# Sigmoid attention with its keys in chunks of 128 and the last 64 of two pairs taken together

## The chip, the cores and the metric

The kernel runs on one core of a Trainium2 chip. The metric is device time in microseconds (us) of one execution; 1193.59 us is the median of three runs of the kernel before. Engines are named as the profile names them: PE (matmul), PEld (its weight loads), DVE, ACT, POOL, and SP, which here only issues DMAs. SPq and ACTq are the DMA issues of SP and ACT.

## What is computed

```python
# q, k, v: (4, 12, 448, 64) fp32
scores = (q @ k.transpose(0, 1, 3, 2)) / sqrt(64) - log(448)
attn   = 1 / (1 + exp(-scores))
x      = (attn @ v), heads side by side         # (4, 448, 768)
# first block, weights float64
u  = x + (x.T @ U @ V).T                         # rank 32 over the 448 positions
x  = u + relu(u @ w_ch1) @ w_ch2                 # 768 -> 3072 -> 768
# second block
t  = x @ w_theta
u  = x + w_tok_r @ (x * cos(t)) + w_tok_i @ (x * sin(t))
out = u + relu(u @ w_ch)
```

## The kernel before

The result stays in SBUF as `X`, transposed (feature on the partition). Nearly every product is made of three matmuls of two-part fp32r numbers (high by high, high by low, low by high); the attention's weights times values, the U product and the transposes are plain fp32.

**Attention.** The 48 heads are taken as 24 pairs, p = 0 to 23, six to a batch. The loop over p is written out by hand, and every engine gets its instructions in that order. For pair p it does: scores `QK(p, 0)` and `QK(p, 1)`, two chunks of 112 keys each; for each chunk six matmuls, two heads on the two halves of PE's rows, and one sigmoid on ACT (tile `A`). Between them stand `AV(p-1, c)`, weights times values of the pair before (fp32, two heads on the two halves of PE's columns, four chunks, one PSUM accumulator `av`), the transposes `TK`, `TQ` of the next pair's k and q on DVE with their splits (`kh`, `kl`, `qh`, `ql`), `XN(p-2)`, which turns a finished pair of `X` for the rank-32 product, and after each sixth pair `U1` (that product) and then `U2` (its second half, two matmuls for a PSUM tile `h` and one addition into `X`, in three of the next six iterations).

**Loads.** At the end of iteration p SP gets the loads of pair p+4's k and q (four DMAs each, because each is loaded as four sets of 32 x 32 squares, `load_squares`) and of pair p+3's v (two DMAs). Only the very first q and the first two v go by ACT's queue. Each DMA waits for the landing of the DMA that stands eight places before it in the program (eight completion counters are dealt in turn, over both queues), and its buffer must be free.

**Weights.** They come as float64, are loaded as 32-bit words by SP (tile `ws`), and `Conv` makes two fp32r parts of them in steps: `size` on ACT, `shift`, `sign`, `low` on DVE, then `fin` (a copy on ACT, `ca_w` and `w` on POOL). Nine conversions are dealt into the attention loop (`early_step`), the rest into the mixer (`place`, `tick`).

**The rest** is the channel mixer `ch1`/`ch2` over 12 blocks of 256 hidden features and four batches, then the second block: 5,000 matmuls of 384 or 448 columns in a row.

Of the kernel before, what the change touches and what calls it, by code (L numbers as in the profile page):

```python
# [24 lines left out]
def tile_kernel(  # L25
# [88 lines left out]
    def add_pool(o, a, b):  # L114
        nc.gpsimd.tensor_add(o, a, b)

# [10 lines left out]
    class Conv:  # L127
        def __init__(self, key, pp, n, dma, fin, turns=False, more=()):
            self.key, self.pp, self.n, self.dma = key, pp, n, dma
            self.turns = turns  # L130
# [6 lines left out]
        def load(self):  # L137
            self.S = cv.tile([P, DM, 2], U32, tag="ws", name=f"ws_{self.key}", bufs=3)[:self.pp, :self.n]
            self.hw = self.S[:, :, 1]
            self.dma(self.S)  # L140

        def size(self):
# [3 lines left out]
            nc.scalar.activation(f(self.A), f(self.hw), AF.Abs, scale=65536.0)  # L146

        def shift(self):
            A = self.A
            nc.vector.tensor_scalar(  # L150
                out=f(A), in0=f(A), scalar1=2.0, scalar2=1.875 * 2.0 ** 32, op0=ALU.max, op1=ALU.min
            )
            nc.vector.tensor_scalar(
                out=A, in0=A, scalar1=4, scalar2=1, op0=ALU.logical_shift_left, op1=ALU.logical_shift_right
            )

        def sign(self):
            A, hw = self.A, self.hw
            nc.vector.scalar_tensor_tensor(
                out=A, in0=hw, scalar=0x80000000, in1=A, op0=ALU.bitwise_and, op1=ALU.bitwise_or  # L160
            )
            nc.vector.tensor_scalar(out=hw, in0=A, scalar1=0xFF800000, scalar2=None, op0=ALU.bitwise_and)

        def low(self):
            A, e = f(self.A), f(self.hw)
            c = 2.0 ** -52 * (INV_HI if self.turns else 1.0)
            nc.vector.scalar_tensor_tensor(
                out=e, in0=self.S[:, :, 0], scalar=c, in1=e, op0=ALU.mult, op1=ALU.mult
            )
            if self.turns:  # L170
                nc.vector.scalar_tensor_tensor(
                    out=e, in0=A, scalar=INV_LO, in1=e, op0=ALU.mult, op1=ALU.add
                )
                nc.scalar.activation(A, A, AF.Copy, scale=INV_HI)
# [6 lines left out]
    def split(o, a, e, eng=nc.gpsimd):  # L181
        hi_act(o[:, 0], a)
        eng.tensor_sub(a, a, f(o[:, 0]))  # L183
        eng.tensor_add(o[:, 1], a, e)  # L184

    def fin_split(dest, key, name, tag):
        def fin(a, e):
            dest[key] = ring(tag, name)
            split(dest[key], a, e)
# [28 lines left out]
    def conv_kept(name, src, kk, turns):  # L218
        st = {}

        def fin(a, e):
            st["o"] = spill_tile(name).rearrange("p (a n) -> p a n", a=2)
            split(st["o"].bitcast(F32R), a, e, nc.vector if turns else nc.gpsimd)
# [11 lines left out]
    def conv_tok(i):  # L235
# [17 lines left out]
        def fin(a, e):  # L253
            st["t"] = spill_tile(f"tok{i}")
            st["n"] = st["t"][:CP, 2 * S:2 * S + NC * P]
            add_pool(st["n"], a, e)
# [12 lines left out]
        return Conv(f"tok{i}", CP, NC * P, dma, fin, False, [turn, spill])  # L269

    def conv_U():
        def dma(s):
            sv = s.rearrange("p (a c r) t -> p a c (r t)", a=2, c=NC)
            for par in range(2):
                for c in range(NC):
                    for n, t, m in runs(par, c * CP, (c + 1) * CP):
                        o = n - c * CP
                        nc.sync.dma_start(out=sv[o:o + m, par, c], in_=U_w[t:t + m, :])

        def fin(a, e):  # L280
            add_pool(u_in.rearrange("p a c r -> p (a c r)"), a, e)
        return Conv("U", CP, 2 * NC * R, dma, fin)

    def conv_V(par):
# [8 lines left out]
        def fin(a, e):  # L293
            o = vcat[:, par]
            hi_act(o, a)
            for g in (1, 3):
                sl = slice(g * R, (g + 1) * R)
                lo_pool(a[sl], a[sl], o[sl])
                add_pool(o[sl], a[sl], e[sl])
# [12 lines left out]
    u_in = ap.tile([CP, 2, NC, R], F32, name="u_in")  # L312
    vcat = ap.tile([P, 2, S], F32R, name="vcat")

    q_t, k_t, v_t, qq_t, kk_t, A_t, av_t, xn_t = {}, {}, {}, {}, {}, {}, {}, {}
# [22 lines left out]

    def load_v(p, eng=nc.sync):
        b, hp = divmod(p, NH)  # L340
        vt = ap1.tile([CP, 2, NC, D], F32, tag="v", name=f"v_{p}", bufs=4)
        for h in range(2):
            eng.dma_start(out=vt[:, h], in_=v[b, 2 * hp + h].rearrange("(c p) d -> p c d", p=CP))
        v_t[p] = vt

    def TQ(p):
# [8 lines left out]
        else:  # L355
            hi_act(h_, x)
        qq_t[p] = (h_, l_)
        return lambda: lo_dve(l_, x, h_)

    kT_t = {}  # L360
# [12 lines left out]
    def K_lo(p):  # L373
        h_, l_ = kk_t[p]
        lo_dve(l_, kT_t.pop(p), h_)

    def QK(p, half):


        (kh, kl), (qh, ql) = kk_t[p], qq_t[p]  # L380
        for c in (2 * half, 2 * half + 1):
            ps = ps_b.tile([P, 2, 512], F32, tag="sc", name=f"sc_{p}_{c}", bufs=2)
            for n, (a, b) in enumerate(((kh, qh), (kh, ql), (kl, qh))):
                for h in range(2):
                    sl = slice(h * D, (h + 1) * D)
                    nc.tensor.matmul(  # L386
                        ps[:CP, h, :S], a[sl, c * CP:(c + 1) * CP], b[sl], start=n == 0, stop=n == 2
                    )
            a = ap1.tile([CP, 2, S], F32, tag="A", name=f"A_{p}_{c}", bufs=6)
# [565 lines left out]
```

## Time and profile before

| | |
|---|---|
| timed runs | 1192.83, 1193.59, 1193.81 us |
| the profiled execution | 1195.51 us, of which its span in the trace is 1193.6 us |
| granted clock of PE, mean | 0.998 |
| PE busy | 1177.1 us, 99% of the span |
| DVE, ACT, POOL busy | 783.5, 377.4, 298.1 us |
| DMA, attention stage | 0.73 of the 16 engines' time from 20 to 160 us |

The attention stage ends at about 192 us. A busy PE in the profile is not PE at its peak, since matmuls overlap; how far apart they start tells more than how long one takes.

### The profile page before, as it was taken

The page shows a single profiled execution, that of the slowest core. Times are in us where ns is not written, and L with a number is a line of the kernel's source. Part 1 is how long each engine was busy: PE and PEld are TensorE (multiplying, and loading weights), DVE is VectorE, ACT ScalarE, POOL GpSimd, SP SyncE. Part 2 cuts the span into 40 slices and gives each one's busy share as a digit, 9 for nine tenths or more (in the row PEclk, how much of TensorE's full clock was granted, in tenths as well). Part 3 has the DMA queues.
Part 4 walks back from the last instruction along what each step waited for, and adds up shares of the span by engine and source line. Part 5 has one row for each costly group of instructions (what it writes and reads, how often), then busy time and mean ns, then how long its engine had stood idle before and what let it go on. Part 6 is the DMA issues. An engine that isn't in the chain of part 4 may idle for free.

```text
span 1193.6 us, 15586 instructions
## 1 busy us (share of the span) xinstructions
PE 1177.1 (99%) x6220; PEld 1016.0 (85%) x6220; DVE 783.5 (66%) x955; ACT 377.4 (32%) x498; POOL 298.1 (25%) x170
## 2 busy tenths in 40 slices
PE   8989999999999999999999999999999999999998
PEld 4444446999999999999999999999989999999997
DVE  5578874557786778677867796878574642833443
ACT  6767774212221222221222121212124431631110
POOL 0131212422232233222322242525102421320000
PEclk9999999999999999999999999999999999999999
DMA  8687740011232123212321232324442000030344
GB/s 139 118 164 148 154 87 27 1 40 67 95 99 80 53 95 111 69 53 95 110 69 54 95 115 86 118 99 127 188 160 80 1 1 1 2 158 1 51 65 70
DMA packets 190808, 99.88 MB, mean 84 GB/s; under 512 B 158736, under 2 KB 182672, under 8 KB 190608
## 3 DMA queue, kind: packets, MB, share of 16 engines
q1 hardware_dynamic: 164752, 95.45, 28.7%
q10 hardware_dynamic: 25984, 3.44, 2.1%
q8 instruction: 49, 0.80, 0.3%
q14 instruction: 23, 0.19, 0.1%
HBM read 80.71 MB, written 18.15 MB: 83 GB/s over the span
## 4 chain that ended last, share of the span: by engine, by line
PE 90%; DVE 3%; SPq 3%; DMA 2%; ACT 1%; issue 1%; ACTq 0%; DVEq 0%
PE g L626 10%; PE g L627 10%; PE g L628 10%; PE y L648 10%; PE y L650 10%; PE y L649 10%; PE av L399 3%; PE y L837 3%; PE y L838 3%; PE y L836 3%; PE sc L386 3%; PE th L759 2%; PE th L763 2%; PE th L760 2%; PE wc L919 2%; PE wc L917 2%
## 5 line engine op out<-in xcount | busy, mean ns | idle before, releaser
L648 PE MATMUL y<-gh,w 128*128 128x448 f32 x576 | 211.3, 367 | 0.7 <-DVE X L652 0.7
L626 PE MATMUL g<-uh,w 128*128 128x448 f32 x576 | 210.7, 366 | 0.0
L627 PE MATMUL g<-ul,w 128*128 128x448 f32 x576 | 210.5, 365 | 0.0
L650 PE MATMUL y<-gh,w 128*128 128x448 f32 x576 | 210.5, 365 | 0.0
L628 PE MATMUL g<-uh,w 128*128 128x448 f32 x576 | 210.5, 365 | 0.0
L649 PE MATMUL y<-gl,w 128*128 128x448 f32 x576 | 210.4, 365 | 0.0
L652 DVE TENSOR_TENSOR X<-y,X 128x896 f32<-128x896 f32 x144 | 156.4, 1088 | 78.8 <-PE y L650 77.3
L183 POOL TENSOR_TENSOR ca_w<-ca_w,w 128x768 f32<-128x768 f32 x48 | 90.6, 1888 | 456.7 <-ACT w L109 444.2
L633 ACT ACTIVATE gh<-g 128x896 fp32r<-128x896 f32 x48 | 44.2, 920 | 330.7 <-PE g L628 330.7
L634 DVE SCALAR_TENSOR_TENSOR gl<-g,gh 128x896 fp32r<-128x896 f32 x48 | 52.4, 1091 | 100.9 <-ACT gh L633 100.9
L648 PEld LDWEIGHTS y<-gh,w 128*128 128x128 f32 x576 | 108.2, 188 | 9.9 <-issue 1.1
L626 PEld LDWEIGHTS g<-uh,w 128*128 128x128 f32 x576 | 108.2, 188 | 9.1 <-issue 0.4
L650 PEld LDWEIGHTS y<-gh,w 128*128 128x128 f32 x576 | 108.2, 188 | 8.8
L628 PEld LDWEIGHTS g<-uh,w 128*128 128x128 f32 x576 | 108.2, 188 | 8.7
L627 PEld LDWEIGHTS g<-ul,w 128*128 128x128 f32 x576 | 108.2, 188 | 8.7
L649 PEld LDWEIGHTS y<-gl,w 128*128 128x128 f32 x576 | 108.2, 188 | 8.5
L390 ACT ACTIVATE A<-sc,bias_s 112x896 f32<-112x896 f32 x96 | 91.5, 1005 | 22.9 <-PE sc L386 22.7
L184 POOL TENSOR_TENSOR w<-ca_w,ws_w 128x768 fp32r<-128x768 f32 x48 | 96.2, 2004 | 3.8
L399 PE MATMUL av<-A,v 112*64 112x448 f32 x384 | 83.5, 557 | 1.1 <-ACT X L109 1.1
L112 POOL TENSOR_TENSOR zl<-t,zh 128x768 fp32r<-128x768 f32 x23 | 42.7, 1883 | 114.1 <-ACT zh L109 114.1
L146 ACT ACTIVATE ca_w<-ws_w 128x768 f32<-128x768 f32 x48 | 43.5, 906 | 62.3 <-POOL w L184 55.9
L836 PE MATMUL y<-tok,zh 128*128 128x448 f32 x168 | 61.7, 367 | 0.0
(145 smaller groups left out, 1861.6 us busy)
## 6 DMA issues: line engine op xcount, KB each, us to landing
ws_w<-in_moe_w_ch_dram SPq DMA_DIRECT2D x48, 768.0 KB, 4.5
k<-in_k_dram SPq DMA_DIRECT2D x96, 56.0 KB, 2.7
q<-in_q_dram SPq DMA_DIRECT2D x92, 56.0 KB, 2.4
v<-in_v_dram SPq DMA_DIRECT2D x44, 112.0 KB, 2.8
ws_th<-in_moe_w_theta_dram SPq DMA_DIRECT2D x6, 768.0 KB, 4.4
th_d<-sp_th SPq DMA_DIRECT2D x6, 768.0 KB, 6.2
ws_wc<-in_moe_w_ch_dram SPq DMA_DIRECT2D x6, 768.0 KB, 4.5
wc_d<-sp_wc SPq DMA_DIRECT2D x6, 768.0 KB, 7.0
```

The source lines that it names most:

```text
L183: eng.tensor_sub(a, a, f(o[:, 0]))
L184: eng.tensor_add(o[:, 1], a, e)
L390: nc.scalar.activation(a, ps[:CP, :, :S], AF.Sigmoid, bias=bias_s[:CP], scale=SCALE)
L399: nc.tensor.matmul(ps[h * D:(h + 1) * D, :S], v_t[p][:, h, c, :], A_t[p, c][:, h, :], start=c == 0, stop=c == NC - 1,)
L626: nc.tensor.matmul(o, wh[:, sl], uh_t[b][:, kk, :], start=kk == 0, stop=False)
L627: nc.tensor.matmul(o, wh[:, sl], ul_t[b][:, kk, :], start=False, stop=False)
L628: nc.tensor.matmul(o, wl[:, sl], uh_t[b][:, kk, :], start=False, stop=kk == NK - 1)
L648: nc.tensor.matmul(o, wh[:, sl], gh[:, j, :], start=j == 0, stop=False)
L649: nc.tensor.matmul(o, wh[:, sl], gl[:, j, :], start=False, stop=False)
L650: nc.tensor.matmul(o, wl[:, sl], gh[:, j, :], start=False, stop=j == FB - 1)
L652: nc.vector.tensor_add(x, ps[:, :, :S], x)
L836: nc.tensor.matmul(o, zh[:, sl], tok_h[:, i, :], start=n == 0, stop=False)
```

## The change

The keys are cut at 0, 128, 256 and 384. The three full chunks are made as before, with 128 keys instead of 112 (`QK(p, c)`, `AV(p, c)`, c = 0 to 2). The last 64 keys of an even pair and of the odd pair after it are taken together. `QK_rest(m)` makes their scores with four fp32 matmuls of 64 rows by 64 columns, one on each quarter of PE (head by row half, output by column half), directly from `kT` and `qT`, into two banks of one score tile; one sigmoid does for both pairs (tile `AL`). `AV_rest(m)` multiplies them by the values, again four matmuls on the four quarters, and ends the even pair's sum and begins the odd pair's, so `av` has two buffers. `ux` shrinks to one bank for that, and `U2` is done one half at a time, at two places (`U2_one`). v is loaded as 128 x 3 rows (`v`) and 64 rows (`vl`), each head by itself: four DMAs for a pair instead of two. U is loaded in seven DMAs instead of nine. The conversion of weights makes 24-bit numbers in three steps on DVE (`bits`, `top`, `word`), without POOL's addition at the end, and in the attention loop the low part is subtracted on DVE instead of POOL. The long runs of matmuls in the mixer and the second block stay.

```diff
     class Conv:
...
-            self.steps = [self.size, self.shift, self.sign, self.low, lambda: fin(f(self.A), f(self.hw)), *more]
+            self.steps = [self.size, self.bits, self.top, self.word, *([self.finish] if fin else []), *more]
...
-            nc.scalar.activation(f(self.A), f(self.hw), AF.Abs, scale=65536.0)
...
+            nc.scalar.activation(f(self.A), f(self.S[:, :, 1]), AF.Copy, scale=2.0 ** -112)
+
+        def bits(self):
+            lw = self.S[:, :, 0]
+            nc.vector.tensor_scalar(out=lw, in0=lw, scalar1=2.0 ** -29, scalar2=7.0, op0=ALU.mult, op1=ALU.min)
+
+        def top(self):
+            A, lw = self.A, self.S[:, :, 0]
+            nc.vector.scalar_tensor_tensor(
+                out=lw, in0=A, scalar=0x80000000, in1=lw, op0=ALU.bitwise_and, op1=ALU.bitwise_or
             )
...
+        def word(self):
+            A, lw = self.A, self.S[:, :, 0]
+            nc.vector.scalar_tensor_tensor(
+                out=A if self.dest is None else self.dest(), in0=A, scalar=3, in1=lw,
+                op0=ALU.logical_shift_left, op1=ALU.bitwise_or,
             )
...
     def load_v(p, eng=nc.sync):
         b, hp = divmod(p, NH)
-        vt = ap1.tile([CP, 2, NC, D], F32, tag="v", name=f"v_{p}", bufs=4)
+        vt = ap1.tile([P, 2, NFULL, D], F32, tag="v", name=f"v_{p}", bufs=4)
+        if p % 2 == 0:
+            vl_t[p // 2] = ap1.tile([P, 2, D], F32, tag="vl", name=f"vl_{p // 2}", bufs=3)
         for h in range(2):
-            eng.dma_start(out=vt[:, h], in_=v[b, 2 * hp + h].rearrange("(c p) d -> p c d", p=CP))
+            eng.dma_start(
+                out=vt[:, h], in_=v[b, 2 * hp + h, :NFULL * P].rearrange("(c p) d -> p c d", p=P)
+            )
+        for h in range(2):
+            eng.dma_start(out=vl_t[p // 2][half(p, h), p % 2], in_=v[b, 2 * hp + h, NFULL * P:])
...
+    def QK_rest(m):
+
+        ps = ps_b.tile([P, 2, 512], F32, tag="sc", name=f"sl_{m}", bufs=2)[:, :, :S]
+        for x in range(2):
+            for h in range(2):
+                sl = slice(h * D, (h + 1) * D)
+                nc.tensor.matmul(
+                    ps[half(x, h), x], kT_t[2 * m + x][sl, NFULL * P:], qT_t[2 * m + x][sl], start=True, stop=True
+                )
+        AL_t[m] = weigh(ps, "AL", f"AL_{m}", 1)
...
+    def AV_rest(m):
+        for x in range(2):
+            ps = av_out(2 * m + x)
+            for h in range(2):
+                r = half(x, h)
+                nc.tensor.matmul(
+                    ps[h * D:(h + 1) * D, :S], vl_t[m][r, x], AL_t[m][r, x], start=x == 1, stop=x == 0
+                )
+        av_done(2 * m)
...
     for p in range(NP):
         nx = p + 1 < NP
         QK(p, 0)
+        QK(p, 1)
         if nx:
             TK(p + 1)
             TQ(p + 1)()
...
-        b, r = divmod(p - 3 - NH, NH)
-        if b >= 0 and r < NK // 2:
-            U2(b, 2 * r, ps_a.tile([P, 2, 512], F32, tag="ux", name=f"h_{b}_{r}"), vcat[:, b % 2, :], 2)
-        QK(p, 1)
+        U2_one(p, 0)
+        QK(p, 2)
...
+        if p % 2 == 0:
+            QK_rest(p // 2)
         if p:
             AV(p - 1, 2)
-            AV(p - 1, 3)
+        if p % 2:
+            AV_rest(p // 2)
         u1_lo()
+        U2_one(p, 1)
```

On PE an iteration reads before, here p = 4 (`sc_c` is the score tile of chunk c, `av` the accumulator, `xt` the transposes for `XN`):

```order
L386 MATMUL sc_0_433<-qh_374,kh_383 112x448 x2
L386 MATMUL sc_0_433<-ql_375,kh_383 112x448 x2
L386 MATMUL sc_0_433<-qh_374,kl_384 112x448 x2
...
L399 MATMUL av_459<-A_0_359,v_149 64x448 x2
L399 MATMUL av_459<-A_1_368,v_149 64x448 x2
...
L412 MATMUL xt_490<-ident,X 112x128 x4
L399 MATMUL av_459<-A_2_396,v_149 64x448 x2
L399 MATMUL av_459<-A_3_405,v_149 64x448 x2
```

and after, here the odd p = 3 (rows left out as above):

```order
L405 MATMUL sc_2_469<-qh_376,kh_384 128x448 x2
L405 MATMUL sc_2_469<-ql_377,kh_384 128x448 x2
L405 MATMUL sc_2_469<-qh_376,kl_385 128x448 x2
L455 MATMUL xt_478<-ident,X 128x128 x4
L431 MATMUL av_457<-A_2_396,v_154 64x448 x2
L443 MATMUL av_457<-AL_410,vl_155 64x448 x2
L443 MATMUL av_488<-AL_410,vl_155 64x448 x2
```

An iteration loses one chunk of scores (three rows) and one of `av`; each odd one gains the two last rows, and each even one two such rows for `sl`, the scores of the rest, behind `xt`.

On SP the loads of two iterations read before (`k`, `q`, `v` with a running number, four or two DMAs to a row):

```order
L325 DMA k_954<-in_k_dram 32x14x32 x4
L325 DMA q_955<-in_q_dram 32x14x32 x4
L343 DMA v_964<-in_v_dram 112x4x64 x2
L325 DMA k_1039<-in_k_dram 32x14x32 x4
L325 DMA q_1040<-in_q_dram 32x14x32 x4
L343 DMA v_1049<-in_v_dram 112x4x64 x2
L194 DMA ws_w_0_1_1092<-in_moe_w_ch_dram 128x1536
```

and after:

```order
L331 DMA k_924<-in_k_dram 32x14x32 x4
L331 DMA q_925<-in_q_dram 32x14x32 x4
L355 DMA v_934<-in_v_dram 128x3x64 x2
L359 DMA vl_830<-in_v_dram 64x64 x2
L331 DMA k_1008<-in_k_dram 32x14x32 x4
L331 DMA q_1009<-in_q_dram 32x14x32 x4
L355 DMA v_1018<-in_v_dram 128x3x64 x2
L359 DMA vl_1019<-in_v_dram 64x64 x2
L190 DMA ws_w_0_1_1024<-in_moe_w_ch_dram 128x1536
```

Each pair has twelve DMAs in place of ten; the weights' loads (`ws_w`) keep their places between the pairs.

On ACT the start of the program holds, after the change:

```order
L331 DMA q_101<-in_q_dram 32x14x32 x4
L572 ACT_TABLE_LOAD
L572 ACTIVATE warm<-bias_s 128x1
L355 DMA v_111<-in_v_dram 128x3x64 x2
L359 DMA vl_112<-in_v_dram 64x64 x2
L355 DMA v_117<-in_v_dram 128x3x64 x2
L359 DMA vl_112<-in_v_dram 64x64 x2
L109 ACTIVATE kh_199<-kT_197 128x448
```

Eight issues for the v of pairs 0 and 1, where there were four, stand ahead of the first work on k (`kh`).

## Rows read from the trace of the kernel before

**Rows 1.** Windows: busy time of each engine by stretch (x instructions), clock, DMA

```profile
20.00:160.00 140.00, 135.50 (x884) 66.25 (x884) 103.27 (x180) 104.05 (x141) 28.57 (x19) 0.99 0.73 143
...
192.00:1193.00 1001.00, 995.66 (x5044) 925.35 (x5042) 647.96 (x722) 239.93 (x311) 264.02 (x143) 1.00 0.24 75
```

**Rows 2.** Timeline of PE, one iteration: start, time, instruction

```profile
104.47 0.46 PE L386 MATMUL sc<-qh,kh 64*112 64x448 f32 x2
104.77 0.36 PE L386 MATMUL sc<-ql,kh 64*112 64x448 f32 x2
104.97 0.36 PE L386 MATMUL sc<-qh,kl 64*112 64x448 f32 x2
...
105.88 1.72 PE L399 MATMUL av<-A,v 112*64 112x448 f32 x8
107.54 0.46 PE L386 MATMUL sc<-qh,kh 64*112 64x448 f32 x2
...
108.95 0.65 PE L412 MATMUL xt<-ident,X 128*112 128x128 f32 x4
109.53 1.72 PE L399 MATMUL av<-A,v 112*64 112x448 f32 x8
111.18 0.46 PE L386 MATMUL sc<-qh,kh 64*112 64x448 f32 x2
```

**Rows 3.** Timeline of SP's queue: issue, time for all of the row

```profile
122.26 2.00 SPq L325 DMA_DIRECT2D k<-in_k_dram  x4
...
126.44 0.96 SPq L343 DMA_DIRECT2D v<-in_v_dram  x2
127.49 0.43 SPq L194 DMA_DIRECT2D ws_w<-in_moe_w_ch_dram  x1
```

**Rows 4.** Waits from 0 to 190 us: total, times, longest

```profile
DVE kT L364 <- DMA k<-in_k_dram: 12.3, 5, 4.8
DVE qT L350 <- DMA q<-in_q_dram: 10.2, 7, 2.8
```

**Rows 5.** DMA issues from 20 to 160 us: count, KB each, us to landing

```profile
v<-in_v_dram SPq DMA_DIRECT2D x42, 112.0 KB, 2.8
...
k<-in_k_dram SPq DMA_DIRECT2D x80, 56.0 KB, 2.7
q<-in_q_dram SPq DMA_DIRECT2D x80, 56.0 KB, 2.4
```

**Rows 6.** Timeline of SP's queue behind a load of weights (91.47 us)

```profile
91.47 0.42 SPq L194 DMA_DIRECT2D ws_w<-in_moe_w_ch_dram  x1
...
93.98 4.71 SPq L325 DMA_DIRECT2D q<-in_q_dram  x4
```

**Rows 7.** Timeline of SP's queue, the last q load

```profile
155.92 2.17 SPq L325 DMA_DIRECT2D q<-in_q_dram  x2
```

**Rows 8.** Timeline of DVE, 166 to 178 us

```profile
170.83 0.95 DVE L159 SCALAR_TENSOR_TENSOR ca_w<-ws_w,ca_w 128x768 uint32<-128x768 uint32 x1
...
175.98 0.66 DVE L350 STREAM_TRANSPOSE qT<-q 128x64 f32<-128x64 f32 x2
```

**Rows 9.** Timeline of PE, the last pair and the mixer's first matmul

```profile
179.87 0.46 PE L386 MATMUL sc<-qh,kh 64*112 64x448 f32 x2
...
182.94 0.68 PE L448 MATMUL h<-vcat,pc 128*128 128x448 f32 x2
183.54 0.46 PE L386 MATMUL sc<-qh,kh 64*112 64x448 f32 x2
...
188.31 3.23 PE L399 MATMUL av<-A,v 112*64 112x448 f32 x16 [1.05 <-ACT X L109]
...
191.87 0.45 PE L626 MATMUL g<-uh,w 128*128 128x448 f32 x1
```

**Rows 10.** Timeline of ACT, the start

```profile
4.43 1.95 ACTq L343 DMA_DIRECT2D v<-in_v_dram  x4
6.42 0.58 ACT L109 ACTIVATE kh<-kT 128x448 fp32r<-128x448 f32 x1 [2.12 <-DVE kT L364]
```

More of the change, by code (lines that the diff above doesn't have):

```diff
@@ L219, in conv_kept, with fin @@
         st = {}
-        def fin(a, e):
+        def fin(a, t):
             st["o"] = spill_tile(name).rearrange("p (a n) -> p a n", a=2)
-            split(st["o"].bitcast(F32R), a, e, nc.vector if turns else nc.gpsimd)
+            o = st["o"].bitcast(F32R)
+            if turns:
+                split_turns(o, a, t)
+            else:
+                split(o, a, lo_pool)
         def spill():
@@ L268, in spill @@
             nc.sync.dma_start(out=tok_d[:, :, i, :], in_=st["o"])
-        return Conv(f"tok{i}", CP, NC * P, dma, fin, False, [turn, spill])
+        return Conv(f"tok{i}", CP, NC * P, dma, None, False, [turn, spill], dest)
     def conv_U():
@@ L273, in dma, with put, dest @@
             sv = s.rearrange("p (a c r) t -> p a c (r t)", a=2, c=NC)
+            def put(o, i):
+                nc.sync.dma_start(out=o, in_=i)
             for par in range(2):
[L275 to L282, printed above, removed]
+                for c0, n0, n1 in ((0, 0, P), (1, P, NFULL * P), (NFULL, S - P, S)):
+                    for n, t, m in runs(par, n0, n1):
+                        if m > P:
+                            put(sv[:, par, c0:NFULL], U_w[t:t + m, :].rearrange("(c p) w -> p c w", p=P))
+                        else:
+                            put(sv[n - n0:n - n0 + m, par, c0], U_w[t:t + m, :])
+        def dest():
+            return u_in.rearrange("p a c r -> p (a c r)").bitcast(U32)
+        return Conv("U", P, 2 * NC * R, dma, None, dest=dest)
     def conv_V(par):
@@ L374, in K_lo @@
         h_, l_ = kk_t[p]
-        lo_dve(l_, kT_t.pop(p), h_)
-    def QK(p, half):
-        (kh, kl), (qh, ql) = kk_t[p], qq_t[p]
[L381 to L389, printed above, removed]
-            nc.scalar.activation(a, ps[:CP, :, :S], AF.Sigmoid, bias=bias_s[:CP], scale=SCALE)
-            A_t[p, c] = a
+        lo_dve(l_, kT_t[p], h_)
@@ new lines, in weigh, with QK @@
+    def weigh(ps, tag, name, bufs):
+        a = ap1.tile([P, 2, S], F32, tag=tag, name=name, bufs=bufs)
+        nc.scalar.activation(a, ps, AF.Sigmoid, bias=bias_s, scale=SCALE)
+        return a
+    def QK(p, c):
+        ps = ps_b.tile([P, 2, 512], F32, tag="sc", name=f"sc_{p}_{c}", bufs=2)[:, :, :S]
+        (kh, kl), (qh, ql) = kk_t[p], qq_t[p]
+        for n, (a, b) in enumerate(((kh, qh), (kh, ql), (kl, qh))):
+            for h in range(2):
+                sl = slice(h * D, (h + 1) * D)
+                nc.tensor.matmul(ps[:, h], a[sl, c * P:(c + 1) * P], b[sl], start=n == 0, stop=n == 2)
+        A_t[p, c] = weigh(ps, "A", f"A_{p}_{c}", 5)
@@ L497, in place_extra @@
             at(i, b, t, name)
-        at(*((i, b + 1, 0) if job.turns else (i, b, 4)), name)
+        if job.fin:
+            at(*((i, b + 1, 0) if job.turns else (i, b, 4)), name)
         at(i, b + 1, 2 if job.turns or b + 1 == B else 0, name)
-        for t in range(len(job.steps) - 5):
+        for t in range(len(job.steps) - (5 if job.fin else 4)):
             at(i, b + 1, 3 + t, name)
@@ L536, in tile_kernel @@
     load_v(2)
-    esteps = [j for j in early for _ in range(5)]
+    esteps = [j for j in early for _ in j.steps]
     def early_step():
@@ L566, in tile_kernel, with U2_one @@
     lo_q()
+    def U2_one(p, n):
+        b, r = divmod(p - 3 - NH, NH)
+        if b >= 0 and r < NK // 2:
+            ps = ps_a.tile([P, 512], F32, tag="ux", name=f"h_{b}_{r}_{n}")
+            U2(b, 2 * r + n, ps.rearrange("p (a n) -> p a n", a=1), vcat[:, b % 2, :])
     for p in range(NP):
@@ L653, in ch2 @@
             after(e2)
-    for c in range(NC):
+    for c in range(NFULL):
         AV(NP - 1, c)
```

101 lines of the change are left out of this document (47 added, 54 removed).

## Prediction

> **What bounds the kernel now.** First the windows by stage. From 192 us on PE is busy for 995.66 of 1001 us [rows 1]: this stage is nothing but PE, and its matmuls are not changed, so nothing that the new conversion saves on DVE and POOL there (648 and 264 us of 1001) can show. All that counts is when the mixer's first matmul starts, at 191.87 us [rows 9]. From 20 to 160 us PE is busy for 135.5 of 140, DVE and ACT for 103 and 104, the DMA engines for 0.73. The timeline of one iteration shows PE without a gap: 104.47 to 111.18, 6.71 us for a pair [rows 2].
>
> That is one bound. Another runs beside it. SP issues ten DMAs for a pair in 122.26 to 127.49, 5.23 us or 0.523 each [rows 3], whatever their size. With what else it issues it needs nearly PE's pace, and the waits show that it is felt: DVE, which turns k and q, sat idle for 12.3 and 10.2 us because they had not landed [rows 4]. The timeline of SP's queue has no gap from 20 to 158.09 us, when the last pair's q is issued (155.92 + 2.17) [rows 7]. In these 138.1 us it issues 80 k, 80 q, 40 v (of the 42; the last two come after) [rows 5], 6 loads of weights and 21 of U and V (9 and 12 by the code): 227 issues at 0.523 are 118.7 us. The other 19.4 us are issues that last longer than that. One such row: the q behind a load of weights took 4.71 us [rows 6] where four take 2.0 [rows 3]. So SP is never idle; what it has in hand at the end is a lead. The last q is in SBUF at about 160.5 (its issue and the median 2.4 us to land [rows 5]) and is turned at 175.98 [rows 8]: 15.5 us of lead.
>
> **PE, part by part.** Six pairs of score matmuls take 105.88 - 104.47 = 1.41 us, a pair 0.20 (104.77 to 104.97); two chunks of `av` 107.54 - 105.88 = 1.65; `XN` 109.53 - 108.95 = 0.58 [rows 2]. Before: 2 x 1.41 + 2 x 1.65 + 0.58 = 6.70. After, the scores are 1.41 + (1.41 - 3 x 0.20) = 2.22, the values 1.65 + 0.83 = 2.48, `XN` 0.58, and one group of four quarter matmuls in each iteration (scores in even ones, values in odd ones). No row shows four at once. The nearest are two at once: `av`'s two heads, fp32 over 448 columns, one chunk 0.83. If the four run side by side like those two, a group costs 0.83 to 0.90 (a chunk that stands alone pays more of the start); if two by two, 1.66; one by one, 3.3. Nothing would be below the 0.83 of one chunk, since each quarter streams the same 448 fp32 columns. I take 0.90: 6.18 us, 0.52 saved for a pair, 12 us over 23 iterations. `U2` in two halves costs something back: two matmuls take 183.54 - 182.94 = 0.60 [rows 9], one alone, with a start and an end of its own, I estimate at 0.40, so 0.2 x 9 = 1.8. Left: about 10 us, if PE alone set the pace.
>
> **SP.** Two more DMAs for a pair stand ahead of every later k and q. Before the last q are the v of pairs 2 to 21: 20 x 2 x 0.523 = 20.9 us. U has two DMAs fewer, -1.0. At the start ACT issues eight v DMAs instead of four ahead of `kh`: four took 1.95, and `kh` began at 6.42, right behind them [rows 10], so `kh` is 2.0 us later; SP's second pair waits for completion counters that these v now hold, by the same 1 to 2 us, and I take 1.3 for SP. What the issues that last longer will do is the unknown. The lower end of their cost is nothing (then 19.4 us are gained), the upper end the same 19.4 (the same weights, with the same eight k and q DMAs right behind each). I take 5.5 saved, because the nearest row has the excess, 2.7 us, directly behind the weights, where nothing changes; only what the transfers before left over gets less, as the same bytes are spread over a longer time. Sum: 20.9 - 1.0 + 1.3 - 5.5 = +15.7 us, against a lead of 15.5. So the last q is turned at about 176.2 instead of 175.98: the lead is used up exactly, and SP, not PE, sets the pace of the loop.
>
> **The end.** From there to the mixer's first matmul it was 191.87 - 175.98 = 15.9 us. The last pair loses 0.61 of scores and one `av` chunk more or less: behind `U2` the two groups of `av` are 0.83 + 0.90 instead of 1.65 (+0.1), `U2` costs +0.2, the last pair's own `av` three chunks instead of four (-0.8; 3.23 for four [rows 9]). Sum -1.1. So 176.2 + 15.9 - 1.1 = 191.0, 0.9 us earlier than before. The v of the last pair must land before the odd pair's rest. It is issued behind the last q, nine issues later (4.7 us), so at about 181; with 2.8 to 5 us to land that is 184 to 186, and PE gets there about 188: hidden, by little.
>
> **What costs nothing.** The conversion's DVE work: 0.56 to 0.95 for each operation of 768 columns [rows 8], one or two fewer in each conversion, one subtraction more in the loop, where POOL (28.6 us of 140) loses as much [rows 1]. DVE has 37 us idle of these 140, and a slower loop gives it more. If SP were not the bound, DVE with 103 us in a loop shortened by 10 would still have 27. ACT has three and a half sigmoids for a pair instead of four, and had 36 us of 140 idle [rows 1]. `TK` of every second pair must now wait until the scores of the rest have read `kT`; they stand an iteration ahead, so I count nothing; if it weren't hidden it would be a part of 0.9 us in every second iteration.
>
> Against the profiled execution: 1193.6 of span and 1195.51 of time; the timed runs have a median 1.9 us lower, which I carry over. 1193.6 - 0.9 gives 1192.7, said as 1192.5. A run of this kernel tells 0.2%, 2.4 us, from no change, and no less.
>
> **The rivals.** (a) *Faster*: the long issues behind the weights mostly go, since the DMA engines' 0.73 falls to about 0.65. With all 19.4 us gone SP would be done 14 us sooner than in the sum above, PE's 10 us would come out, less the 2 of the start: 183.9, 1185.5 us. Half of it gone gives 187 to 188, 1189. For it: the engines are not full on the mean. Against it: the excess lies in bursts behind the weights, which stay. Chance 0.37 for more than 2.4 us.
>
> (b) *Slower*: the quarters don't run together. The price is 0.83 for each turn more. SP's pace with the change is (158.09 + 15.7 - 20) / 20 = 7.7 us for a pair, PE's 6.7 with `U1` and `U2`; so one more turn is nearly hidden (+1 to +4 us at the end), and from two more on PE is the bound again: 6.18 + 1.66 = 7.8, 1.1 above the old 6.7, 23 times, or 25 us: 1193.6 + 25 = 1219. The trace has two heads on two column halves into one bank (`av`) and two heads on two row halves into two banks (`sc`), both side by side; it has no two row halves writing to one bank, which the rest's scores and values both do. The Trainium skill, "TensorEngine Tiling (Array Packing)", section "Restrictions and Gotchas", says of just this: "Different row tiles cannot access same PSUM bank simultaneously". By that rule the two heads of a pair take turns and the four need two to three turns; with two, the sum would come out some 3 us higher, with three it would be the 1219 above; by the trace as far as it goes (halves at full pace) it stays. Chance 0.08 for two turns more, 0.1 for one.
>
> (c) *Slower, by SP*: the long issues stay as they are (+5.5), or the start costs SP more than 1.3. Then the last q is turned at 181.7 and the end is 196.5: 1198. Every microsecond of SP beyond the lead is one at the end. For it: the completion counters reach over only eight issues. Chance 0.17, so that (b) and (c) are slower together by 0.25.
>
> (d) *No change beyond 2.4 us*: the sum above, 0.38, from 1191.2 to 1196.0.
>
> **Range.** The end of (a) at 1185 and of (c) at 1199 leave about 2 in 10 out. Faster 0.37, same 0.38, slower 0.25; the case's own range is 1190 to 1196.
>
> **What would show it.** SP's queue without a gap to about 174 us, and the last q turned right after it lands, with no lead: right. Iterations of PE at 6.2 us where they have no gap, and gaps whose end is DVE's turning of k or q, so that `kT` and `qT` wait for DMA for far more than 22 us: right. Wrong for PE: starts of a quarter group more than 0.1 us apart; PE without gaps. Wrong for SP: the last q at 160 to 168 us. Wrong for all of it: a difference behind 192 us, where the matmuls are the same.

## The result and the profile after

The changed kernel takes 1203.27 us, the median of four runs (1203.02 to 1203.58), against 1193.7 us of the kernel before beside it. The ratio is 1.0071, with an interval of 1.0057 to 1.0084: slower, and outside the range of the prediction. The profiled span is 1201.4 us, before 1193.6: 7.8 of the 9.6 us, because the profiled execution of before took 1195.51 us, 1.8 above its median. The span splits at the mixer's first matmul:

| | before | after | forecast |
|---|---|---|---|
| last `q` issued by | 158.09 | 179.21 | 173.8 |
| last `q` turned on DVE | 175.98 | 181.41 | 176.2 |
| mixer's first matmul | 191.87 | 196.33 | 191.0 |
| from there to the end of the span | 1001.73 | 1005.07 | 1001.7 |

So 4.5 us are lost ahead of the mixer and 3.3 us behind it. First the windows by stage of the changed kernel, the answer to [rows 1] (columns as there):

```profile
20.00:160.00 140.00, 130.59 (x818) 56.85 (x816) 92.47 (x170) 92.67 (x127) 0.00 (x0) 0.96 0.63 125
...
197.00:1201.00 1004.00, 998.84 (x5040) 924.77 (x5039) 523.66 (x594) 233.82 (x304) 155.16 (x88) 1.00 0.24 75
```

Every engine works less in the loop, PE too (130.59 us of 140 for 135.5), DMA fell to 0.63 as forecast, and still the loop is longer: what bounds it is none of the busy engines. The granted clock is 0.96 for 0.99. An iteration without a gap, on PE's timeline, answers to [rows 2]:

```profile
104.74 0.47 PE L405 MATMUL sc<-qh,kh 64*128 64x448 f32 x2
...
106.16 1.72 PE L431 MATMUL av<-A,v 128*64 128x448 f32 x8
107.81 0.47 PE L405 MATMUL sc<-qh,kh 64*128 64x448 f32 x2
...
108.62 0.66 PE L455 MATMUL xt<-ident,X 128*128 128x128 f32 x4
109.20 0.98 PE L414 MATMUL sl<-qT,kT 64*64 64x448 f32 x8
110.12 0.97 PE L431 MATMUL av<-A,v 128*64 128x448 f32 x4
111.02 0.47 PE L405 MATMUL sc<-qh,kh 64*128 64x448 f32 x2
```

From 104.74 to 111.02 it is 6.28 us, with 0.92 for the group of quarters (109.20 to 110.12) and 0.90 for a chunk of `av` of its own right behind it (110.12 to 111.02). The four quarters take one turn, not two: 15 of the 24 groups in this trace fit into 0.92 us. In six others a part started late because it waited, three times for `qT`, three times for `vl`, which lands too late in this loop; PE's weight loads show the longest of these:

```profile
68.98 0.45 PEld L443 LDWEIGHTS av<-AL,vl 64*64 64x64 f32 x4 [2.18 <-DMA vl<-in_v_dram]
```

SP's queue at its end answers to [rows 7], DVE's turn of the last `q` to [rows 8]:

```profile
173.79 1.13 SPq L359 DMA_DIRECT2D vl<-in_v_dram  x2
175.03 2.09 SPq L331 DMA_DIRECT2D k<-in_k_dram  x4
177.22 1.99 SPq L331 DMA_DIRECT2D q<-in_q_dram  x4
```

```profile
181.41 0.66 DVE L366 STREAM_TRANSPOSE qT<-q 128x64 f32<-128x64 f32 x2
```

The lead of 15.5 us is gone: the last `q` is turned 2.2 us after its issue, which is no more than a load takes to land. DVE's waits up to 190 us say the same, against 12.3 and 10.2 us in [rows 4]:

```profile
DVE kT L381 <- DMA k<-in_k_dram: 28.7, 11, 7.9
...
DVE qT L366 <- DMA q<-in_q_dram: 19.6, 15, 2.1
```

What such a wait does to PE, on its timeline and in the window around it:

```profile
39.67 0.97 PE L414 MATMUL sl<-qT,kT 64*64 64x448 f32 x4
44.83 1.76 PE L414 MATMUL sl<-qT,kT 64*64 64x448 f32 x4 [4.18 <-DVE qT L366]
46.52 1.76 PE L431 MATMUL av<-A,v 128*64 128x448 f32 x4
```

```profile
40.00:50.00 10.00, 5.82 (x24) 0.66 0.54 94
```

The scores of the rest of pairs 4 and 5 need `q` of pair 5 in the middle of pair 4's iteration, half an iteration sooner than the chunks did. PE stands for 4.18 us and then runs at half clock (1.2 GHz): the same `av` chunk takes 1.76 us instead of 0.97. There are three such half-clock stretches up to 100 us (the windows 10 to 20, 40 to 50 and 90 to 100 us show 0.83, 0.66 and 0.83); before there was one (60 to 70 us, 0.83). ACT's start answers to [rows 10]:

```profile
4.46 0.94 ACTq L355 DMA_DIRECT2D v<-in_v_dram  x2
5.44 1.18 ACTq L359 DMA_DIRECT2D vl<-in_v_dram  x2
6.66 1.14 ACTq L355 DMA_DIRECT2D v<-in_v_dram  x2
7.83 1.16 ACTq L359 DMA_DIRECT2D vl<-in_v_dram  x2
9.04 0.58 ACT L109 ACTIVATE kh<-kT 128x448 fp32r<-128x448 f32 x1 [4.73 <-DMA v<-in_v_dram]
```

`kh` starts at 9.04 instead of 6.42, and the first score matmul at 10.13 instead of 7.58. The end answers to [rows 9]; 181.41 to 196.33 is 14.9 us, forecast 14.8:

```profile
193.51 2.48 PE L431 MATMUL av<-A,v 128*64 128x448 f32 x12
...
196.33 0.45 PE L679 MATMUL g<-uh,w 128*128 128x448 f32 x1
```

The 3.3 us behind the mixer's start don't show as idle time: PE is busy throughout in both. They show in how many matmuls fit into a window. One window of PE inside the mixer, of the kernel before, then of the changed one:

```profile
735.00:885.00 150.00, 150.00 (x742) 1.00 0.38 131
```

```profile
735.00:885.00 150.00, 150.00 (x728) 1.00 0.34 116
```

14 matmuls fewer of the same shape at the same full clock. Starts of matmuls stand 202.7 ns apart there before, 206.7 after, on the mean; this distance is called the pitch below. The pitch rises from the one to the other in both kernels when the seventh block of token weights is turned (700 us before, 704 after). Before it falls back at 715 us; after it stays up to 900. PE's timeline of before, then DVE's of before and of after, show the difference:

```profile
714.80 0.37 PE L650 MATMUL y<-gh,w 128*128 128x448 f32 x1
715.01 0.46 PE L648 MATMUL y<-gh,w 128*128 128x448 f32 x1
715.30 0.37 PE L649 MATMUL y<-gl,w 128*128 128x448 f32 x1
```

```profile
710.41 2.53 DVE L167 SCALAR_TENSOR_TENSOR ws_w<-ws_w 128x768 f32<-128x768 uint32 x1
712.85 1.08 DVE L634 SCALAR_TENSOR_TENSOR gl<-g,gh 128x896 fp32r<-128x896 f32 x1
713.86 1.08 DVE L652 TENSOR_TENSOR X<-y,X 128x896 f32<-128x896 f32 x1
```

```profile
715.79 1.09 DVE L687 SCALAR_TENSOR_TENSOR gl<-g,gh 128x896 fp32r<-128x896 f32 x1 [2.39 <-ACT gh L686]
717.31 1.09 DVE L705 TENSOR_TENSOR X<-y,X 128x896 f32<-128x896 f32 x1 [0.44 <-PE y L703]
```

Before, a step of the old conversion (2.53 us) makes `gl` late on DVE, so the addition of the first third of `y` ends at 714.94, and PE's next matmul pair into that bank is some 0.09 us late: 0.29 between two starts instead of 0.20. After, DVE sat idle ahead of `gl` and the addition is done 1.2 us ahead of need. That the short wait is what brings the pitch back was a theory to test.

### The profile page after: what moved, and what is told of

Same layout as the page of the kernel before. It is cut to its first block, busy times and chain, and to the rows that moved or that the text cites. A ratio compares the mean times of both kernels' runs of the same rounds, so it can differ in the third digit from the quotient of the medians.

```text
span 1201.4 us, 15131 instructions
## 1 busy us (share of the span) xinstructions
PE 1179.7 (98%) x6172; PEld 1006.8 (84%) x6172; DVE 650.7 (54%) x828; ACT 361.4 (30%) x480; POOL 155.9 (13%) x94
## 4 chain that ended last, share of the span: by engine, by line
PE 93%; SPq 3%; DVE 1%; DMA 1%; ACT 1%; issue 0%; ACTq 0%; DVEq 0%
PE y L701 10%; PE g L679 10%; PE g L680 10%; PE y L702 10%; PE y L703 10%; PE g L681 10%; PE av L431 4%; PE sc L405 3%; PE y L890 3%; PE y L891 3%; PE y L889 3%; PE th L812 2%; PE th L816 2%; PE th L813 2%; PE wc L971 2%; PE wc L972 2%
## 5 line engine op out<-in xcount | busy, mean ns | idle before, releaser
L112 POOL TENSOR_TENSOR w<-ca_w,w 128x768 fp32r<-128x768 f32 x42 | 77.9, 1854 | 497.0 <-ACT w L109 497.0
L396 ACT ACTIVATE A<-sc,bias_s 128x896 f32<-128x896 f32 x72 | 69.9, 1005 | 24.7 <-PE sc L405 24.4
L431 PE MATMUL av<-A,v 128*64 128x448 f32 x288 | 66.8, 573 | 0.0
L889 PE MATMUL y<-tok,zh 128*128 128x448 f32 x168 | 61.7, 367 | 0.0
L890 PE MATMUL y<-tok,zh 128*128 128x448 f32 x168 | 61.5, 366 | 0.0
L891 PE MATMUL y<-tok,zl 128*128 128x448 f32 x168 | 61.4, 366 | 0.0
L109 ACT ACTIVATE w<-ca_w 128x768 fp32r<-128x768 f32 x48 | 40.3, 840 | 63.8 <-PE y L703 63.8
```

The lines of the kernel that those rows point to most:

```text
L112: nc.gpsimd.tensor_sub(o, a, b)
L431: nc.tensor.matmul(ps[h * D:(h + 1) * D, :S], v_t[p][:, h, c, :], A_t[p, c][:, h, :], start=c == 0 and p % 2 == 0, stop=c == NFULL - 1 and ...
L889: nc.tensor.matmul(o, zh[:, sl], tok_h[:, i, :], start=n == 0, stop=False)
L890: nc.tensor.matmul(o, zh[:, sl], tok_l[:, i, :], start=False, stop=False)
L891: nc.tensor.matmul(o, zl[:, sl], tok_h[:, i, :], start=False, stop=n == NZ - 1)
```

## The experiments

Theory 1 for the stage ahead of the mixer: the issues on SP's queue (with the start, which delays them) set its end. Rivals: the quarters themselves, or what they need early. Theory A for the mixer: a short wait of PE, which the old conversion caused, resets the pitch. Rival: the pitch follows from other work. All ratios are against runs of the kernel before on the same chip, whose medians there were 1195 to 1197 us. Times of the profiled execution, the last but one column being span less mixer's first matmul. Each row is one execution: the changed kernel and hold_once, one_turn_more and turn_at_719 have the same attention stage, and in them the mixer's first matmul comes at 195.56 to 197.42 and SP's first `v` at 20.72 to 22.14, so a difference of 1 to 2 us ahead of the mixer says little by itself:

| run | first score | last `q` turned | mixer's first | to the end | ratio, interval |
|---|---|---|---|---|---|
| v_on_pool | 11.24 | 173.76 | 188.70 | 1005.3 | 0.9986 (0.9973 to 1.000) |
| before_two_more_issues | 7.72 | 182.86 | 198.75 | 1002.1 | 1.0071 (1.0048 to 1.0094) |
| start_v_on_pool | 8.27 | 179.53 | 194.46 | 1004.7 | 1.0040 (1.0027 to 1.0054) |
| rest_rows_joined_hold | 9.14 | 177.20 | 192.12 | 1001.9 | 1.0006 (0.9991 to 1.0020) |
| quarters_undone_v_on_pool | 8.37 | 173.10 | 188.99 | 1004.7 | 0.9999 (0.9982 to 1.0016) |
| before_all_v_on_pool | 8.19 | 173.44 | 189.32 | 1004.8 | 0.9989 (0.9974 to 1.0003) |
| old_conversion | 10.05 | 182.22 | 197.14 | 1002.3 | 1.0050 (1.0031 to 1.0070) |
| new_conversion_alone | 7.65 | 174.35 | 190.27 | 1004.3 | 0.9986 (0.9972 to 1.000) |
| hold_once | 10.18 | 182.50 | 197.42 | 1002.0 | 1.0032 (1.0017 to 1.0046) |
| one_turn_more | 10.16 | 180.62 | 195.56 | 1005.4 | 1.0067 (1.0047 to 1.0087) |
| turn_at_719 | 10.16 | 181.86 | 196.44 | 1005.4 | 1.0054 (1.0036 to 1.0073) |
| all_v_on_pool_hold | 8.07 | 168.03 | 182.97 | 1001.9 | 0.9915 (0.9890 to 0.9941) |

**v off SP's queue** (v_on_pool), on the changed kernel:

```diff
-            load_v(p + 3)
+            load_v(p + 3, nc.gpsimd)
```

> From pair 3 on, the loads of v (two of 128 rows, two of 64 rows a pair) are issued from GpSimd's queue, which is idle in the loop after the change, instead of SyncE's; nothing else changes. Theory 1, SyncE's issues set the pace of the attention stage after the change: 84 issues of 0.52 to 0.63 us leave SyncE, the last q is issued well before 165 us, the stalls of TensorE behind 50 us (1.4, 0.4, 1.6, 0.8, 0.9 and 0.7 us, and one half-clock stretch worth 1.7 us) go, and the mixer's first matmul comes at 187 to 191 us instead of 196.4: 1193 to 1198 us. Rival, the pace is set by the quarter products themselves or by what they need half an iteration early: the first matmul stays at 195 to 197 us, 1202 to 1204 us. Behind the first matmul nothing changes: 1005 us.

Measured: 1193.82 us. SP's last `q` is issued 31 us sooner, and DVE's waits shrink:

```profile
146.03 1.99 SPq L331 DMA_DIRECT2D q<-in_q_dram  x4
```

```profile
DVE kT L381 <- DMA k<-in_k_dram: 12.7, 3, 6.0
...
DVE qT L366 <- DMA q<-in_q_dram: 6.3, 7, 2.0
```

The mixer's first matmul came at 188.70, 7.6 us sooner though the start was 1.1 us later. Theory 1 holds for these 7.6 us: the quarters are the same and need `q` as early. No weight load of PE waits for `vl` any more. A part of the rival stays: from the second pair's `X` on ACT to the fourth pair's it takes 17.9 us here, 20.1 in the changed kernel, 13.4 before, because the rest of pairs 4 and 5 still waits for `q` (2.87 us at 43.74), with a half-clock stretch behind it (0.66 from 40 to 50 us).

**The issues alone** (before_two_more_issues), on the kernel before, from pair 2 on:

```diff
+        if p > 1:
+            xt = ap1.tile([P, D], F32, tag="vx", name=f"vx_{p}", bufs=3)
+            for h in range(2):
+                eng.dma_start(out=xt[h * D:(h + 1) * D], in_=v[b, 2 * hp + h, NFULL * P:])
```

> The kernel before, with two more small loads a pair on SyncE's queue (the last 64 rows of v again, into a tile that nothing reads) from pair 2 on: the price of the issues alone, without the change. Theory 1: 44 issues of 0.55 to 0.63 us add 24 to 28 us to SyncE's queue, which had a lead of about 15.5 us: the last q is turned 8 to 12 us later than 175.98 us, and the time is 1200 to 1206 us. Rival, SyncE's issues were hidden and the change's loss lies in the quarters: within 2 us of 1193.7 us.

Measured: 1204.1 us, as much as the whole change costs, from loads that nothing reads. The last `q` was turned 6.9 us later (8 to 12 expected), right after it landed:

```profile
171.78 1.14 SPq L347 DMA_DIRECT2D vx<-in_v_dram  x2
173.02 2.09 SPq L325 DMA_DIRECT2D k<-in_k_dram  x4
175.21 1.99 SPq L325 DMA_DIRECT2D q<-in_q_dram  x4
```

Two of these loads take 1.24 us to the next row's start, 0.62 each. Summed from start to start over all of SP's queue, the 40 ahead of the last `q` took 26.2 us, 0.65 each, and the last issue came 19 us later, some 7 us less than that, because the other rows got shorter.

**The start alone** (start_v_on_pool), on the changed kernel:

```diff
-    load_v(0, nc.scalar)
-    load_v(1, nc.scalar)
+    load_v(0, nc.gpsimd)
+    load_v(1, nc.gpsimd)
```

> The changed kernel with the eight loads of v for the first two pairs on GpSimd's queue instead of ScalarE's. The prediction put the start's later first score matmul to the two more issues of 64 rows a pair ahead of ScalarE's rounding of k. If that holds, the first score matmul falls from 10.4 us to 7 to 8 us. As SyncE's issues set the end of the loop, the rest of the time follows SyncE's queue alone: the last q is turned 0 to 2.5 us earlier than 181.7 us, by the gap in SyncE's queue ahead of the first q of pair 1 that this removes; 1200.5 to 1203.3 us. Rival, the start sets the pace of everything behind it: the time falls by the whole 2.5 to 3 us, to 1200 us, with the last q turned at 179 us.

Measured: 1201.26 us; the first score matmul is 1.9 us sooner (8.27, for 7 to 8 expected), and so are the last `q` (1.9) and the mixer's first matmul (1.9). What the start loses seems kept to the end, as its rival said; but by way of SP, whose first `v` starts at 20.38 instead of 22.14. The two theories differ little here, and 1.9 us is no more than the attention stage scatters by itself. The timed runs put the term at 2 us (1201.26 for 1203.27) to 4 us (by the ratios, 1.0040 for 1.0071).

**Fewer issues without another queue** (rest_rows_joined_hold), with the hold that is told below:

```diff
-        for h in range(2):
-            eng.dma_start(out=vl_t[p // 2][half(p, h), p % 2], in_=v[b, 2 * hp + h, NFULL * P:])
+        if p % 2 == 0:
+            h0 = 2 * hp
+            for o, hs in ((0, slice(h0, h0 + 4, 3)), (REM, slice(h0 + 1, h0 + 3))):
+                eng.dma_start(
+                    out=vl_t[p // 2][o:o + REM], in_=v[b, hs, NFULL * P:].rearrange("x p d -> p x d")
+                )
```

> The changed kernel with the last 64 rows of v of two pairs in two loads (64 rows of two heads each) instead of four, all on the queues where they were, and with VectorE held up once at 717.5 us as in the run with one hold. Theory 1, the number of issues on SyncE's queue sets the end of the attention stage: 20 issues of 0.65 us fewer on SyncE (13 us) and two fewer at the start on ScalarE (some 1.3 us): the last q is issued at 163 to 167 us instead of 179, the queue has a lead again, and the mixer's first matmul comes at 186 to 190 us, as with v on GpSimd's queue; from there 1002 us with the pitch back at 202.6 ns: 1188 to 1193 us. Rival, the loop with v on SyncE's queue is held by the landing and the completion counters of v, not by the number of issues, or a load of two heads costs twice as much to issue: the first matmul stays at 194 to 196.5 us and the whole at 1197 to 1199 us.

Measured: 1196.47 us, no difference from before, and a miss of the time. The mixer's first matmul is at 192.12, between the two theories. The joined loads cost little more each:

```profile
130.21 1.26 SPq L361 DMA_DIRECT2D vl<-in_v_dram  x2
131.56 0.55 SPq L331 DMA_DIRECT2D k<-in_k_dram  x1
```

Twenty of them, from start to start, are 14.8 us instead of 25.9, yet the last `q` is issued only 5.6 us sooner, 1.1 of them from the start: the rows of `k`, `q` and `v` took 7.3 us more in sum. SP's queue is not a sum of fixed prices. When one load goes, part of its time turns up in the others' rows; what they wait for then was not told apart.

**Without the quarters, SP relieved** (quarters_undone_v_on_pool: the kernel before with the new conversion, all four `load_v` calls on `nc.gpsimd`; before_all_v_on_pool: the same with the old conversion).

> The kernel before with the new conversion and with all loads of v on GpSimd's queue, in chunks of 112: against the run with all v on GpSimd's queue it is the change without its quarters, at a SyncE queue that binds neither. Theory 1, the quarters give what the iterations show (6.28 against 6.71 us, some 0.43 us in each of about 22 iterations, 8 to 10 us) and SyncE's queue took it away: with SyncE relieved this kernel gains at most 2 us, since TensorE bounds it, and the mixer's first matmul comes at 187.5 to 191 us against 182.2: with the pitch of 206.7 ns behind 700 us 1192 to 1196 us in all. Rival, the quarters are worth nothing and all of the gain came from the relieved queue: first matmul at 181 to 184 us, 1186 to 1189 us.

> The kernel before with all loads of v on GpSimd's queue, nothing else: does SyncE's queue bound the kernel before as well? Theory 1: no, it had a lead of about 15.5 us; TensorE bounds the loop, and the waits of its start and middle (1.07 us at 12 us, 2.6 us at 62 to 65 us) may shrink: first matmul of the mixer at 188 to 192 us, the whole 1190 to 1194 us. GpSimd also works on the conversion here, so a load of v can wait behind its operations of 2 to 4 us; four buffers of v cover that. Rival: the queue did bind, and the first matmul comes at 182 to 186 us, 1184 to 1188 us.

Measured: 1196.14 and 1194.62 us. With SP relieved the old chunks fill PE; its window from 20 to 160 us:

```profile
20.00:160.00 140.00, 139.36 (x935) 1.00 0.83 148
```

The mixer's first matmul comes at 188.99 and 189.32, against 182.97 with the quarters (the last run below), but these 6.0 us are not the worth of the quarters. 3.6 of them are there when ACT writes the first pair's `X` (24.58 against 21.02): from 10 to 20 us the two runs with the old chunks are partly at half clock (0.71 and 0.67), the one with the quarters is not (1.00):

```profile
10.00:20.00 10.00, 6.36 (x32) 0.71 1.13 188
```

Whether the old chunks cause that, or only these executions, is not shown. Behind the first pair the quarters gain 2.5 us in all: they lose 2.1 between the second and the fourth pair, where they wait for `q`, and gain 3.9 from there to the last. 22 iterations shorter by 0.43 would be 9; PE still has gaps (busy for 134.63 us of the window in the last run below, for 139.36 here), and there it waits 2.5 us for the sigmoid of the rest and 1.6 for the additions of `U2`.

The kernel before gains 2.6 us ahead of the mixer from the relief (before_all_v_on_pool): it is 3.5 us later at the first pair's `X` (24.15 for 20.62, with the half-clock stretch), gains 6.4 between the fourth pair's and the eighth's, where PE had waited and run at half clock, and nothing behind these (some 76 us). From there on PE bounded it, as the prediction said; before that SP's queue cost it waits, too. None of this shows in the time: before_all_v_on_pool takes 1004.8 us behind the mixer's start instead of 1001.73, since the pitch there is 206.7 ns from 202 to 346 us.

**The old conversion in the changed kernel** (old_conversion): the class `Conv`, its `fin` functions and their places as before, all else changed.

> The changed kernel with the weights' conversion of before (five steps, with GpSimd), and all the rest of the change. Two theories on the 3.2 us that the change costs behind the mixer's first matmul. Theory A, it comes from the conversion: VectorE, less busy, no longer holds TensorE up for a moment at about 720 us, and without that moment TensorE stays at a pitch of 206.7 ns a matmul instead of 202.6 until 900 us; with the old conversion the pitch falls back at about 720 us and the stretch from the mixer's first matmul to the end is 1001.5 to 1002.5 us. Theory B, it comes from what the attention stage leaves behind (order or alignment of the program): it stays 1005 us. The attention stage itself: first matmul at 195 to 199 us. Sum by A 1198 to 1202 us, by B 1202 to 1205 us.

Measured: 1201.51 us, and 1002.3 behind the mixer's start, with 742 matmuls in the window from 735 to 885 us. The reverse, **the new conversion in the kernel before** (new_conversion_alone):

> The kernel before with only the new conversion of the weights (three steps, no GpSimd in it), chunks of 112 and all else as before. Theory A (the pitch): without VectorE's late addition the pitch stays at 206.7 ns from 705 to 893 us, and from the mixer's first matmul to the end it takes 1004.5 to 1005.5 us instead of 1001.8. In the attention stage the conversion takes less of VectorE and none of GpSimd, and four steps of two jobs instead of five move weights' loads up in SyncE's queue: first matmul of the mixer at 189.5 to 192 us (before 191.87). Sum 1194.5 to 1197.5 us. Rival (no effect behind the mixer's start): 1191 to 1194 us.

Measured: 1195.48 us, 1004.3 behind the mixer's start, and 190.27 for its first matmul. Of the 3.3 us, 2.8 go with the old conversion and 2.6 come with the new one, so they belong to the conversion, in both directions. Ahead of the mixer the kernel before is 1.6 us sooner with the new conversion, which is within the scatter.

**One short wait** (hold_once), on the changed kernel, in `ch2`:

```diff
+            if (i, b, e2) == (8, 2, 0):
+                nc.vector.tensor_copy(ps[:, :, :S], ps[:, :, :S])
+                nc.vector.tensor_copy(ps[:, 0, :256], ps[:, 0, :256])
             nc.vector.tensor_add(x, ps[:, :, :S], x)
```

> The changed kernel with VectorE held up once: ahead of the addition of the first third of the mixer's output at about 717.5 us it copies that third in place (896 and 256 columns, some 1.4 us), so that TensorE, which has about 1.2 us to spare there, waits once for some 0.1 to 0.4 us at 720 us. Theory A, a short wait of TensorE brings the pitch of the matmuls behind it back from 206.7 to 202.6 ns, as the 0.09 us wait did in the kernel before and the 0.06 us wait with the old conversion: from the mixer's first matmul to the end 1002.0 to 1002.6 us, the whole 1200.2 to 1201 us. Rival, the pitch follows from the conversion's work beside it: 206.7 ns stays behind the wait, 1005.2 to 1005.8 us, the whole 1203.4 to 1204 us.

Measured: 1200.32 us. PE's timeline around the wait, and the window behind it:

```profile
720.48 0.37 PE L703 MATMUL y<-gh,w 128*128 128x448 f32 x1
721.25 0.44 PE L701 MATMUL y<-gh,w 128*128 128x448 f32 x1 [0.40 <-DVE X L708]
721.52 0.37 PE L702 MATMUL y<-gl,w 128*128 128x448 f32 x1
```

```profile
735.00:885.00 150.00, 150.00 (x742) 1.00 0.35 120
```

A wait of 0.4 us gives back 3.1 us (1002.0 for 1005.07). The conversion's own work is as in the changed kernel, so the rival falls: theory A holds at this place. In all 14 kernels here the pitch is 206.7 ns behind the seventh turn; it falls to 202.7 between 706 and 722 us in the seven where PE is late once there without added transposes, and in none of the others. But it is no rule that a wait resets the pitch. The kernel before has another wait near the mixer's end,

```profile
893.52 0.45 PE L648 MATMUL y<-gh,w 128*128 128x448 f32 x1 [0.72 <-DVE X L652]
```

and behind it the pitch is 206.2, up from 202.7; with a shorter wait at 900 us the changed kernel stays at 206.7, while turn_at_719, with the same wait, goes down to 202.7.

**A turn more** (one_turn_more at the hook of `(9, 0)`, turn_at_719 at that of `(8, 3)`):

```diff
             tick(i, b, e2 + 2)
+            if (i, b, e2) == (8, 3, 1):
+                ps = ps_g.tile([P, 2, 512], F32, tag="g", name="turn_more", bufs=2)
+                for c in range(NC):
+                    nc.tensor.transpose(ps[:, 0, c * CP:(c + 1) * CP], ident[:CP, :P], ident[:CP, :CP])
```

> The changed kernel with four more transposes of TensorE (of the identity, read by nothing) at about 719 us, in the place that a turn of a token block would have if there were an eighth. In the trace each odd turn lifts the pitch of the matmuls behind it from 202.6 to 206.7 ns, each even one brings it back, and the seventh is the last. Theory A (the pitch is a state that such a break switches): 202.6 ns from 720 us to 893 us, a gain of 3.2 us less 0.4 us for the four and up to 0.7 us for a wait at 893 us that comes back: 1200.4 to 1201.2 us. Rival, the pitch is set by the work beside it (VectorE, transfers): 206.7 ns stays and the time is 1203.3 to 1203.8 us.

> The changed kernel with four more transposes at 719 us, one output of 36 matmuls' length (14.9 us) behind the seventh turn of a token block, which is where an eighth would stand; the earlier run with such a turn had it 30 us behind the seventh. Theory A with places: the second turn of a pair brings the pitch back by where it stands, so 202.6 ns from 719 to 893 us and 1000.4 us less in all than without: 1200.4 to 1201.4 us for the whole. Rival, only a wait of TensorE brings it back, and the earlier second turns did so by a wait that they held: 206.7 ns stays, 1203.3 to 1203.8 us.

Measured: 1203.36 and 1202.54 us, 1005.4 us behind the mixer's start in both: the pitch stayed at 206.7. In the first the transposes came at 734 us, not 719 as its expectation says; the second put them where an eighth turn would stand (the 1000.4 us in its expectation is a slip for 2 to 3). So it is not every second break that brings the pitch back. Nor does each odd turn lift it, as the first expectation says: in both kernels it is 202.7 ahead of the first turn and behind the first and the second; the third, fifth and seventh lifted it, the fourth and sixth brought it back. Why this is so remains open.

**All together** (all_v_on_pool_hold): all `load_v` on `nc.gpsimd`, and the hold.

> The changed kernel with all loads of v on GpSimd's queue (start and loop) and VectorE held up once at the same place as in the run with one hold. If the three causes add: the loop's 8.6 us less by the run with v on GpSimd's queue from pair 3 on, 2 to 3 us of the start, 2.8 us of the pitch: first score matmul at 7 to 8 us, first matmul of the mixer at 184.5 to 187 us, the whole 1186.5 to 1190 us, faster than before. Rival, the start's gain is lost again at the first waits for q behind it (pair 5's q at 43 us is late by SyncE, not by the start): first matmul of the mixer stays at 187 to 188.5 us, the whole 1190 to 1191.5 us.

Measured: 1187.43 us, 0.85% faster than before, and sooner at the mixer (182.97) than the 184.5 to 187 of the sum. Its window from 20 to 160 us has PE at full clock where the changed kernel had 0.96:

```profile
20.00:160.00 140.00, 134.63 (x902) 1.00 0.83 148
```

With the longest of the waits the half-clock stretches went too.

## Why the prediction was wrong

Its frame was right: two bounds side by side, and SP's queue taking over once its lead is used up. The points, one by one:

- **PE's iteration, right; its sum over the loop, too large.** 6.28 us for a forecast of 6.18, the quarter group 0.92 for 0.90. But of the "about 10 us, if PE alone set the pace" the run with SP relieved shows some 4 behind the fourth pair: the waits for the sigmoid of the rest, for the additions of `U2` and for an earlier `q` were not counted. Rival (b) is out: heads on two row halves write to one bank and still take one turn. Quarters that start more than 0.1 us apart, its sign, do occur, but by the waits named above. The Trainium skill's sentence that it weighed ("TensorEngine Tiling (Array Packing)", "Restrictions and Gotchas") is not borne out here, with 0.92 us where two turns would be 1.66. Another page of the Trainium skill, "TensorE: Matmul & The Clock Gate", section "Part 3: Packing small matmuls", has packed matmuls run at the same time, with starts some 4 ns apart; the row agrees that they run together, with four in 0.92 us where two take 0.90 and the four starts within 0.02 us.
- **SP's term, mis-sized: the step that failed ahead of the mixer.** It put the last `q`'s issue 15.7 us later; it came 21.1 us later. "20 x 2 x 0.523 = 20.9" measured 25.9 (25.7 to 26.5 in the three other runs with this attention stage): the 64-row loads take 0.65 from start to start, not the 0.523 of the other rows, so "whatever their size" was wrong. The start, taken as 1.3, was 2.1 by SP's first `v` (22.14 for 20.04; 0.7 to 2.0 in those three). U gave 0.7 for 1.0. The remaining 6.2 us fewer (7.0 fewer in the rows of `k`, `q` and `v`, 0.8 more in those of weights) answer to the 5.5 taken for the long issues. With the lead at zero in the sum, these 5.4 us went to the end almost whole: 181.41 is rival (c)'s 181.7, and 196.33 its 196.5. That (c) has the number is luck: the long issues did get shorter, as the sum had it, and most of the difference was the price of the new loads.
- **The end, right.** 14.9 us from the last `q` to the mixer's first matmul, forecast 14.8. The "about 181" for the last `v` adds its 4.7 us to the turn of the last `q` (176.2) instead of to its issue (173.8), which would give 178.5; it changes nothing, since it landed at 187.67 and PE needed it at 192.20.
- **The mixer, failed.** "Nothing that the new conversion saves on DVE and POOL there (648 and 264 us of 1001) can show": it showed, as the second cause, with 3.3 us. DVE's saving showed as a loss, because one wait of 0.09 us that PE had owed to the old conversion's work had brought PE back to the quicker pitch. The trace of before held both pitches (before and behind 715 us); busy shares, which the prediction read, can't tell them apart.
- **What was not counted:** half-clock stretches, three instead of one, and that the rest's scores need the next pair's `q` half an iteration sooner. In v_on_pool two of the three stretches are still there (0.83 from 10 to 20 us, 0.66 from 40 to 50); in all_v_on_pool_hold none is.

The 0.17 for rival (c) rested on the long issues and the start. That the new loads could have a price of their own was not among its cases, although no row of before shows a load of that shape from SP.

## What to carry to other kernels

When a change adds small transfers to a queue that is never idle, compare its added time with the queue's lead at the end, price the new transfers by rows of their own kind, and move them to a queue that the change has freed before judging the rest of the change. A stage in which an engine is busy all the time can still change its length: count its instructions in a fixed window of both traces.

## What the runs showed of the hardware

- Matmuls of one shape, back to back at full clock, run at either of two pitches, 202.7 or 206.7 ns between starts on the mean. A break (four small transposes, a wait) can switch from one to the other, and the pitch then stays for hundreds of matmuls. A wait of 0.4 us or of less than 0.1 us brought back the quicker one at 720 us, four added transposes did not, and a wait of 0.7 us at 893 us led to the slower one. What decides it is open.
- A load kept SP's queue for 0.50 to 0.53 us with 128 partitions of 768 bytes, for 0.62 to 0.65 with 64 partitions of 256 bytes and for 0.68 to 0.74 with 64 of 512: neither the bytes nor the partitions alone order these.
- Four 64 x 64 quarters of TensorE, with two row halves into one bank, take 0.92 us together where none of them waits, a chunk of two halves 0.90.
